# An adaLN transformer block on one core: conditioning vector loaded first, exponential table loaded early, one query in another PSUM bank, and one small task moved from head 17 to head 31

## Chip, cores, metric

The kernel runs on one core of a Trainium2 chip. The metric is the device time of one execution in microseconds. Each comparison with the kernel before is made on one chip, in the same rounds. "Clock" is the mean granted share of TensorE's clock over the run, rounded to three places: one stretch of 3.4 us at half clock makes it 0.999.

## The reference

```python
mod = silu(c) @ w_mod                     # c: (1, 1024); six vectors of 1024
sa, ca, ga, sb, cb, gb = ...
h = layernorm(x) * (1 + ca) + sa          # x: (2048, 1024), bf16
x = x + ga * attention(h)                 # 32 heads of 128, 4 kv heads, last 512 keys
h = layernorm(x) * (1 + cb) + sb
x = x + gb * swiglu(h)                    # 1024 -> 3584 -> 1024
```

## The kernel before

TensorE works through 4 chunks of 512 rows; in each chunk it makes the query of every head (8 matmuls), its scores (4), and scores times V (16), then the output projection in 8 pieces of 32 matmuls, and at the end the feed-forward part. Heads are counted through all chunks, 32 to a chunk, and the query of head `i + LEAD` (`LEAD` is 3) is made beside head `i`. VectorE copies results out of PSUM, ScalarE takes exponentials. Small jobs ("background tasks": layer norm of the next chunk, broadcasts of a vector into rows) are Python generators that advance one step per head. A tracker puts in the semaphore waits, per PSUM bank and per tile.

The opening. The vector `c` is the third transfer on SyncE's queue; its transpose is TensorE's first instruction:

```python
for t in range(TPC):                       # 4 tiles of x, on two queues in turn
    q = Q_xa[t // 2] if t % 2 else Q_x[t]
    T.op(q, lambda: (A if t % 2 else SP).dma_start(x_res[:, t, :], ...))
    if t == 2:
        T.op(Q_c, lambda: SP.dma_start(c_row[:, :], ...))
...                                        # (cut) weight transfers on SyncE
T.op(PE, ... TE.transpose(bank_bf(XB)[:, 0:DT], c_row, ident))
T.op(ACT, ... A.activation(sc_bf, ..., AF.Silu))
...                                        # (cut) statistics and normalised tiles
warm(9, WB); x_first(0); warm(4, WB); x_first(1)    # warm: matmuls on zeros
...                                        # (cut) modulation, x_first(2), x_first(3)
x_mod()                                    # cast of the modulation, scaled copies into hT
```

The first four queries are computed before the shift of the layer norm is known (a vector; VectorE's cast of it at 26.09 us in before); its contribution is a bias, summed up in bank 2 (`SCB + 2`) by one-column matmuls. The queries lie in `QB0 = [5, 6, 0, 4]`; the scores use banks 0 to 3, later queries bank 4 (`QB`), scores times V banks 5 and 6 (`PVB`), the small tasks and every second output-projection piece bank 7 (`XB`):

```python
T.op(DVE, ... V.tensor_copy(bq, psap((SCB + 2) * 512, ...)))  # copy the biases out of PSUM
q_out(0)               # VectorE: bank 5 + bq[0] -> query 0
q_out(2, True)         # ScalarE: bank 0 + bq[2] -> query 2
q_out(3, True)         # ScalarE: bank 4 + bq[3] -> query 3
for dt in range(5, DT): shift(dt)          # VectorE
q_out(1)               # VectorE
...
if i == 17:
    bg.insert(0, row_task(sc_row, B_scr, sc_bf[:, :], B_sc))
if i == 5:
    add_ln1(1)
...
if (i + LEAD) % Hq == 0:
    finish(ln1[(i + LEAD) // Hq])          # run background steps until it is done
qproj(i + LEAD)                            # always into bank QB
...
def oproj(ch):
    for k in range(2 * TPC):
        b = [QB, XB][k % 2]
        oproj_mm(ch, k, b, 0, Hq)          # 32 matmuls
        oproj_end(ch, k, b)                # two VectorE operations, then run_bg(1)
```

`row_task` has three steps: scale four identity tiles on POOL; four matmuls of 128 columns into bank 7 and a copy on VectorE; the same again for the second half.

The softmax here doesn't subtract the row's maximum and nothing guards it: scores larger than these inputs give would overflow.

## Time and profile before

| what | value | from |
|---|---|---|
| time | 1281.59 us median of 4 (1280.76 to 1282.10) | runs |
| matmuls on TensorE | 1267.8 of 1278.9 us, 99% | page |
| wait for the vector `c` | 6.0 us | chain |
| first scores of head 0 start | 28.68 us | timeline |
| wait before the sixth query | 0.56 us | timeline |
| distance of two query casts at the end of chunk one | 4.46 us; elsewhere 3.50 | timeline |

The first lines of the page of before: span, and busy time of each engine with its share of the span.

```profile
span 1278.9 us, 17849 instructions
...
PE 1267.8 (99%) x7650; PEld 644.5 (50%) x7650; DVE 477.3 (37%) x884; ACT 339.5 (27%) x383; POOL 41.8 (3%) x102
```

The chain of work that ended last in before, in order of time (start us, duration us, what). It shows the few places in which something other than TensorE sets the time.

```profile
1.64 4.35 DMA c_row<-in_c_dram
5.99 0.05 issue
6.04 0.18 PE ps L395
...
15.77 0.18 DVE mod_bf L470
...
27.60 0.16 DVE bq L670
27.76 0.02 issue
27.78 0.76 DVE arena L664
28.55 0.14 issue
28.68 2.76 PE ps L268 x12
31.45 0.02 issue
31.47 0.70 DVE arena L611
...
32.22 3.67 PE ps L268 x28
...
130.00 0.69 DVE arena L712
130.69 0.33 DVE arena L420
```

The vector lands at 5.99. The modulation is cast at 15.77; I use that cast as the mark for the end of the opening. The bias copy (27.60) and query 0 (27.78) release the first scores at 28.68. The cast of the fifth query (31.47) holds the sixth (32.22), which needs the same bank. At 130.69 a modulation of the layer norm holds the first query of chunk two.

VectorE's timeline of before around that last place (start, us, engine, line, operation, output<-input, count, and in brackets the idle time before):

```profile
128.01 0.69 DVE L611 CAST arena<-ps 128x512 bf16<-128x512 f32 x1 [0.17 <-PE ps L268]
...
130.60 1.38 DVE L420 TENSOR_SCALAR arena<-arena,gain,mod_bf 128x512 bf16<-128x512 bf16 x4
132.47 0.69 DVE L611 CAST arena<-ps 128x512 bf16<-128x512 f32 x1 [0.48 <-PE ps L268]
```

Four modulations (L420) come in one lump, and the query casts (L611) are 132.47 - 128.01 = 4.46 us apart. TensorE's wait for them shows as only 0.46 us of idle time; after it, three matmuls start 0.32 us apart instead of 0.216, in step with the remaining modulations.

ScalarE's timeline of before where the first exponential is:

```profile
27.78 1.26 ACT L661 ACTIVATE arena<-ps,bq 128x512 bf16<-128x512 f32 x2 [0.35 <-DVE bq L670]
29.07 1.28 ACT L691 ACT_TABLE_LOAD   x1
30.36 2.14 ACT L691 ACTIVATE arena<-ps 128x1024 bf16<-128x1024 f32 x2
```

### The profile page before, as it was taken

What the parts mean: (1) busy time and instruction counts of PE and PEld (TensorE: products, weight loads), DVE (VectorE), ACT (ScalarE), POOL (GpSimd) and SP (SyncE); (2) the same over time, 40 slices, a digit from 0 to 9 for tenths busy, and PEclk for the clock granted to TensorE, in tenths of its full rate; (3) what the DMA queues carried; (4) which work ended last, traced back from release to release, by engine and by line L of the source; (5) the groups of instructions that cost most, each with busy time, mean ns of one, the idle gap of its engine ahead of it and who ended that gap; (6) DMA issues with size and microseconds to landing.
All of it is one profiled execution on the core that took longest, in us unless ns stands there. A gap on an engine that the chain in (4) does not pass through costs nothing.

```text
span 1278.9 us, 17849 instructions
## 1 busy us (share of the span) xinstructions
PE 1267.8 (99%) x7650; PEld 644.5 (50%) x7650; DVE 477.3 (37%) x884; ACT 339.5 (27%) x383; POOL 41.8 (3%) x102
## 2 busy tenths in 40 slices
PE   7999999999999999999999999999999999999999
PEld 4565545655456564455654444444444444444444
DVE  4555324765237652265322321233222331221222
ACT  3555303555025550055510111011100111011100
POOL 1030000000000010000000000000000000000000
PEclk9999999999999999999999999999999999999999
DMA  9999403966008841055352964045421654035200
GB/s 326 227 237 236 104 1 68 204 137 162 9 20 181 158 104 42 1 130 115 71 149 77 292 224 132 19 146 165 134 73 43 198 147 132 17 114 166 67 9 25
DMA packets 234830, 155.31 MB, mean 121 GB/s; under 512 B 129024, under 2 KB 220032, under 8 KB 234752
## 3 DMA queue, kind: packets, MB, share of 16 engines
q1 hardware_dynamic: 176224, 94.93, 30.6%
q10 hardware_dynamic: 58528, 59.25, 14.7%
q8 instruction: 60, 0.98, 0.3%
q14 instruction: 18, 0.15, 0.0%
HBM read 119.54 MB, written 4.19 MB: 97 GB/s over the span
## 4 chain that ended last, share of the span: by engine, by line
PE 99%; DVE 0%; DMA 0%; issue 0%; SPq 0%
PE ps L268 99%; DMA c_row<-in_c_dram 0%; PE ps L272 0%; SPq L307 0%; DVE arena L664 0%; DVE arena L611 0%; DVE arena L712 0%; DVE tmp L731 0%; DVE arena L733 0%; DVE arena L476 0%; DVE arena L420 0%; DVE rl L709 0%; DVE gain L456 0%; PE ps L395 0%; DVE mod_bf L470 0%
## 5 line engine op out<-in xcount | busy, mean ns | idle before, releaser
L268 PE MATMUL ps<-arena 128*128 128x512 bf16 (+1 forms) x7377 | 1263.0, 334 | 2.2 <-DVE arena L664 0.7
L268 PEld LDWEIGHTS ps<-arena 128*128 128x128 bf16 x7377 | 635.2, 98 | 620.6 <-issue 2.8
L691 ACT ACTIVATE arena<-ps 128x1024 bf16<-128x1024 f32 x256 | 261.9, 1023 | 355.2 <-PE ps L268 343.4
L916 ACT ACTIVATE arena<-ps 128x512 bf16<-128x512 f32 x112 | 66.9, 597 | 506.5 <-PE ps L268 506.5
L917 DVE TENSOR_TENSOR arena<-ps,arena 128x512 bf16<-128x512 f32 x112 | 77.4, 691 | 276.2 <-PE ps L268 276.2
L731 DVE TENSOR_TENSOR tmp<-ps,rowb 128x512 f32<-128x512 f32 (+1 forms) x65 | 44.4, 683 | 319.1 <-PE ps L268 319.1
L611 DVE CAST arena<-ps 128x512 bf16<-128x512 f32 x124 | 85.8, 692 | 58.9 <-PE ps L268 58.9
L712 DVE TENSOR_TENSOR arena<-ps,rl 128x512 bf16<-128x512 f32 x128 | 88.5, 691 | 4.4
L709 DVE RECIPROCAL rl<-ps 128x4 f32<-128x4 f32 x128 | 23.4, 182 | 120.4 <-PE ps L268 120.4
L404 DVE BATCH_NORM_STATS2 st<-x_res 128x6 f32<-128x512 bf16 x62 | 42.3, 683 | 4.5 <-DMA x_res<-in_A_x_dram 4.4
L409 POOL TENSOR_SCALAR rstd<-mv 128x1 f32<-128x1 f32 x28 | 6.2, 221 | 920.0 <-DVE mv L408 920.0
L565 DVE SCALAR_TENSOR_TENSOR arena<-arena 128x1024 bf16<-128x1024 bf16 x24 | 29.2, 1215 | 0.0
L733 DVE TENSOR_TENSOR arena<-tmp,x_res 128x512 bf16<-128x512 f32 (+1 forms) x33 | 22.3, 676 | 1.1
L733 DVE TENSOR_TENSOR x_res<-tmp,x_res 128x512 bf16<-128x512 f32 x32 | 22.1, 692 | 1.1
L420 DVE TENSOR_SCALAR arena<-arena,gain,mod_bf 128x512 bf16<-128x512 bf16 x56 | 20.3, 406 | 0.0
L415 DVE TENSOR_SCALAR nsc<-x_res,mv,rstd 128x1024 bf16<-128x1024 bf16 x30 | 16.0, 535 | 0.0
L411 POOL TENSOR_TENSOR rstd<-rstd,mhalf 128x1 f32<-128x1 f32 x28 | 15.8, 564 | 2.3
L580 POOL TENSOR_SCALAR arena<-arena,c 128x128 bf16<-128x128 bf16 x24 | 14.1, 605 | 9.0 <-PE ps L268 8.8
L268 PEld LDWEIGHTS ps<-sc_bf,arena 128*128 128x128 bf16 x192 | 7.2, 96 | 3.2
L268 PE MATMUL ps<-sc_bf,arena 128*128 128x1 bf16 x192 | 7.3, 164 | 0.0
L408 DVE BATCH_NORM_AGGREGATE mv<-st 128x2 f32<-128x12 f32 x28 | 5.8, 209 | 1.0
L395 PE MATMUL ps<-arena,c_row 8*128 8x8 bf16 x1 | 0.2, 181 | 6.0 <-DMA c_row<-in_c_dram 6.0
(52 smaller groups left out, 42.7 us busy)
## 6 DMA issues: line engine op xcount, KB each, us to landing
arena<-in_A_wq_dram SPq DMA_DIRECT2D x31, 1024.0 KB, 5.7
arena<-in_B_w_gate_dram ACTq DMA_DIRECT2D x28, 1024.0 KB, 5.4
arena<-in_B_w_up_dram ACTq DMA_DIRECT2D x28, 1024.0 KB, 8.2
arena<-in_A_wo_dram SPq DMA_DIRECT2D x8, 1024.0 KB, 7.0
arena<-in_B_w_down_dram SPq DMA_DIRECT2D x7, 1024.0 KB, 8.0
out_dram<-arena SPq DMA_DIRECT2D x15, 256.0 KB, 2.0
x_res<-in_A_x_dram SPq DMA_DIRECT2D x3, 1024.0 KB, 6.7
arena<-in_w_mod_dram SPq DMA_DIRECT2D x8, 256.0 KB, 5.9
```

The lines of the kernel that those rows point to most:

```text
L268: T.op(PE, lambda: TE.matmul(out_ap, lhsT, rhs, start=start, stop=stop, skip_group_check=skip), reads=reads, writes=[bank_buf])
L404: T.op(DVE, lambda: V.bn_stats(st_[sl][:, hf * 6:hf * 6 + 6], x_res[:, t, hf * 512:hf * 512 + 512]), reads=[B_x[t]], writes=[B_st[sl]])
L420: T.op(DVE, lambda: V.tensor_scalar(dst[:, dt, :], dst[:, dt, :], gain[gi][:, dt:dt + 1], mod_bf[:, ccol + dt:ccol + dt + 1], op0=ALU.mult ...
L565: T.op(DVE, lambda: V.scalar_tensor_tensor(mt[n % 2], mt[n % 2], 1.0, sc_row, op0=ALU.mult, op1=ALU.mult, accum_out=mcol[:, n:n + 1]), rea ...
L611: T.op(DVE, lambda: V.tensor_copy(qT_s[qs], bank(QB)), writes=[PB[QB], B_qT[qs]])
L691: T.op(ACT, lambda: A.activation(ex_s[es][:, 2 * kp:2 * kp + 2, :], banks2(SCB + 2 * kp), AF.Exp, scale=att_scale), writes=[PB[SCB + 2 * k ...
L709: T.op(DVE, lambda: V.reciprocal(rl[r][:, :].rearrange("p (a b) -> p a b", a=2), psap(PVB * 512 + P, [[512, 2], [130, 2]])), writes=both + ...
L712: T.op(DVE, lambda: V.tensor_tensor(o_s[os_].rearrange("p (a b) d -> p a b d", a=2), psap(PVB * 512, [[512, 2], [130, 2], [1, P]]), rlb, A ...
L731: T.op(DVE, lambda: V.tensor_tensor(tmp[s][:, 0:n], bank(b, n), rowb[ri][:, c0:c0 + n], ALU.mult), reads=[B_row[ri]], writes=[PB[b], B_tmp ...
L733: T.op(DVE, lambda: V.tensor_tensor(dst[:, c0:c0 + n], tmp[s][:, 0:n], x_res[:, t, c0:c0 + n], ALU.add), reads=[B_tmp[s], B_x[t]], writes= ...
L916: T.op(ACT, lambda: A.activation(sg_s[ss], bank(gb), AF.Silu), writes=[PB[gb], B_sg[ss]])
L917: T.op(DVE, lambda: V.tensor_tensor(guT[:, ft, :], bank(ub), sg_s[ss], ALU.mult), reads=[B_sg[ss]], writes=[PB[ub], B_gu[ft]])
```

## The change

The intent is to shorten the opening and to take small waits off TensorE: the vector goes first on ScalarE's queue, with two warm-up matmuls ahead of its transpose; the exponential's table is loaded in a pause of ScalarE; query 0 reads its bias straight from PSUM, ahead of the bias copy; the sixth query goes to bank 5; the row task that is first needed at head 38 starts at head 31 instead of 17.

```diff
-    Q_c = dq("q_c")
+    Q_c = dq("q_c", nc.scalar)
...
+            T.op(Q_c, lambda: A.dma_start(c_row[:, :], ...), writes=[B_cT])
             for t in range(TPC):
...
-                if t == 2:
-                    T.op(Q_c, lambda: SP.dma_start(c_row[:, :], ...), writes=[B_cT])
...            (the transpose of c and its Silu move down, behind two warm-up matmuls)
+            warm(2, WB)
...
+            T.op(ACT, lambda: A.activation(acc[:, 0:1], mhalf[:, 0:1], AF.Exp), ...)
...
-            warm(9, WB)
+            warm(8, WB)
...
             def q_out(h, on_act=False):
-                if on_act:
+                if h == 0:
+                    T.op(DVE, lambda: V.tensor_scalar(qT_s[h], bank(QB0[h]), bank(SCB + 2, 1, 2 * h), None, op0=ALU.add),
+                         writes=[PB[QB0[h]], PB[SCB + 2], B_qT[h]])
+                elif on_act:
...
+            q_out(0)
             T.op(DVE, lambda: V.tensor_copy(bq[:, :], psap((SCB + 2) * 512, ...)), ...)
-            q_out(0)
...
-                if i == 17:
+                if i == 31:
                     bg.insert(0, row_task(sc_row, B_scr, sc_bf[:, :], B_sc))
...
-                    qproj(i + LEAD)
+                    qproj(i + LEAD, PVB if i == 2 else QB)
```

More of the change, by code (lines that the diff above doesn't have):

```diff
@@ L235, in bass_adaLN_cond__sliding_block_cached__swiglu_ffn__prompt_kernel @@
     B_mode = _Buf("mode"); B_modc = _Buf("modc"); B_bq = _Buf("bq"); B_gf = _Buf("gf")
-    B_nm = _Buf("nmean"); B_acc = _Buf("acc")
+    B_nm = _Buf("nmean"); B_acc = _Buf("acc"); B_acc0 = _Buf("acc0")
     B_g = [_Buf("g%d" % i) for i in range(2)]
@@ L304, in _ @@
             Q_xa = [dq("q_xa%d" % i, A) for i in range(2)]
+            T.op(Q_c, lambda: A.dma_start(c_row[:, :], c.rearrange("o (k p) -> (o k) p", p=P)), writes=[B_cT])
             for t in range(TPC):
@@ L307, in _ @@
                 T.op(q, lambda: (A if t % 2 else SP).dma_start(x_res[:, t, :], xf[t * P:(t + 1) * P, :]), writes=[B_x[t]])
-                if t == 2:
-                    T.op(Q_c, lambda: SP.dma_start(c_row[:, :], c.rearrange("o (k p) -> (o k) p", p=P)), writes=[B_cT])
             OFF_WO = 0
@@ L392, in _ @@
             T.op(POOL, lambda: g.memset(v_aug[:, :, P:P + 2], 1.0), writes=[B_va])
-            T.op(PE, lambda: TE.transpose(bank_bf(XB)[:, 0:DT], c_row[:, :], ident[0:DT, 0:DT]),
-                 reads=[B_cT, B_ident], writes=[PB[XB]])
-            T.op(ACT, lambda: A.activation(sc_bf[:, :], bank_bf(XB)[:, 0:DT], AF.Silu), writes=[PB[XB], B_sc])
             B_ns4 = B_ns + [_Buf("ns2"), _Buf("ns3")]
@@ L485, in mod_ca @@
                 mod_mm(wca[k], B_wca[k], k, MCOLS)
+            WB = PVB
+            warm(2, WB)
+            T.op(PE, lambda: TE.transpose(bank_bf(XB)[:, 0:DT], c_row[:, :], ident[0:DT, 0:DT]),
+                 reads=[B_cT, B_ident], writes=[PB[XB]])
+            T.op(ACT, lambda: A.activation(sc_bf[:, :], bank_bf(XB)[:, 0:DT], AF.Silu), writes=[PB[XB], B_sc])
             tl = TPC - 1
@@ L490, in _ @@
                  reads=[B_x[tl]], writes=[B_ns4[tl], B_acc])
-            WB = PVB
             def stats_only(t):
@@ L509, in _ @@
                  reads=[B_x[tl], B_nm], writes=[B_ns4[tl], B_acc])
+            T.op(ACT, lambda: A.activation(acc[:, 0:1], mhalf[:, 0:1], AF.Exp), reads=[B_mh, B_nm], writes=[B_acc0])
             norm(0, 0, 0)
@@ L600, in _, with qproj @@
             Q_tr = [dq("q_tr%d" % i) for i in range(NOS)]
-            def qproj(i):
+            def qproj(i, b=QB):
                 ch, h = divmod(i, Hq)
@@ L607, in qproj @@
                 for kc in range(DT):
-                    mm(bank(QB), wq_s[sl][:, kc, hh * P:(hh + 1) * P], hT[ch % 2][:, kc, :], kc == 0, kc == DT - 1,
-                       [B_wq[sl][kc // HK], B_hT[ch % 2][kc]], PB[QB])
+                    mm(bank(b), wq_s[sl][:, kc, hh * P:(hh + 1) * P], hT[ch % 2][:, kc, :], kc == 0, kc == DT - 1,
+                       [B_wq[sl][kc // HK], B_hT[ch % 2][kc]], PB[b])
                 qs = i % NQT
-                T.op(DVE, lambda: V.tensor_copy(qT_s[qs], bank(QB)), writes=[PB[QB], B_qT[qs]])
+                T.op(DVE, lambda: V.tensor_copy(qT_s[qs], bank(b)), writes=[PB[b], B_qT[qs]])
             QB0 = [PVB, PVB + 1, SCB, QB]
```

## The prediction

> **What bounds it.** TensorE: the page shows its matmuls busy 1267.8 of 1278.9 us (99%) at granted clock 1.0, and the chain that ended last is 99% TensorE. About 11 us are idle, 6.0 of them before the first instruction, a transpose waiting for the conditioning vector. No matmul work is removed, so over 2% (25 us) is out of reach; what counts is starts and stalls of about a microsecond (timelines of before).
>
> **Gains**
>
> 1. Opening. The vector, issued third at 1.64 us, lands at 5.99; first on ScalarE's queue (0.73) it should land near 3. Warm-up starts near 2.2. The row-tile transposes then wait not for TensorE (9.66) but for VectorE's tiles: first ready at 8.03, second at 10.01, fourth at 12.43. The second tile's transposes start near 10.0 instead of 11.1, the scaled copies near 14.7 instead of 15.77: **-1.1**. Input tiles 1 and 3 are issued 0.4 us later, within slack (landed 4.61 and 5.79, needed 6.01 and 6.33). Weights landed early enough (first query weights 13.45).
> 2. Sixth query in its own bank: the 0.56 us wait (in all 31.49 to 32.22) for the cast out of the shared bank goes: **-0.7**.
> 3. Row task away from head 17: it took three background slots from the second chunk's layer norm, so four modulations were forced out at 130.60 and TensorE stalled; two query casts stand 4.46 us apart there instead of 3.50: **-0.95**.
> 4. Exponential table: its 1.28 us load (29.07 to 30.35) leaves the place before the first exponential, but the next scores come at 33 us and would not have waited: **0**. (The Trainium skill, "ScalarE: Activation LUTs", What ACT_TABLE_LOAD costs, gives 1283 ns plus a drain; this trace agrees on 1.28 and shows no drain.)
>
> **Losses**
>
> 5. First query before the bias copy. The first scores write bank 0, which holds the third query; ScalarE evacuates that with the copied bias. The copy ends about 0.78 us later (behind a 0.75 us operation), so bank 0 is free at about 29.2 instead of 28.4; the first query, earlier by 0.19, no longer decides. Scores start near 29.35 instead of 28.68 (before the opening's shift): **+0.65**.
> 6. Row task at head 31: its third step falls after the first of eight output-projection pieces. Its four small matmuls write the bank that the second piece uses; VectorE must first do two residual operations (0.69 each), then the row copy (0.68). TensorE idles from about 155.3 to 157.3 (before's times): **+1.95**, where before has nothing.
>
> **Sum**: -1.1 -0.7 -0.95 +0.65 +1.95, about -0.2: **1281.8 us** against 1282.04; range 1280.2 to 1283.4. Chances: faster by over 2% 0.003, within 2% 0.994, slower 0.003.
>
> **The profile should show** the first transpose near 3 us; scaled copies from 14.4 to 15.0; no wait before the sixth query; the first scores held by ScalarE's bias evacuation of the third query; the table load near 10 us; query casts 3.5 us apart to the end of chunk one; a new 2 us hole after the first output-projection piece, ended by the row copy.
>
> **What would make it wrong.** TensorE now idles about 1.6 us between warm-up and the first row tiles (6.4 to 8.0). In before the clock rose at 9.33 us, 3.3 us after TensorE started. The Trainium skill ("TensorE: Matmul & The Clock Gate", Part 1) tells of a free-running window of about 3.4 us; the trace agrees with that length. Should the window straddle that pause, the opening's matmuls run at half speed and up to 1.5 us of step 1 is lost, differently from run to run. Or input tile 0, alone at first, lands 0.3 us earlier and speeds VectorE's chain. If the row task's third step is cheaper than I reckon, the kernel is 2 us faster.

## The result, and the profile after

The median is 1281.34 us (1280.08 to 1282.21, 4 runs) against 1281.59 us (1280.76 to 1282.10, 4 runs). The ratio is 0.9998 with a 95% interval of 0.9981 to 1.0015. (Ratios are the mean time of one kernel's fast runs over that of the other's of the same rounds, so not quite the ratio of the medians quoted.) The four runs fall on two levels: 1280.08 and 1280.53 at clock 1.0, and 1282.15 and 1282.21 at clock 0.999. The profiled run is one of the latter.

The chain of the profile after, same columns:

```profile
1.76 6.47 DMA x_res<-in_A_x_dram
...
14.54 0.18 DVE mod_bf L464
...
26.37 0.76 DVE arena L661
27.13 0.02 issue
27.15 0.16 DVE bq L674
27.31 0.80 DVE arena L656 x3
28.11 4.34 PE ps L268 x12
...
154.40 0.70 DVE tmp L734
155.10 0.02 issue
155.13 0.69 DVE x_res L736
155.82 0.61 DVE arena L588
156.43 0.05 issue
156.48 1121.15 PE ps L268 x6360
```

The opening ends at 14.54 instead of 15.77. The bias copy now comes behind query 0 (27.15 behind 26.37). The first scores start only 0.59 us earlier than in before, and then 12 matmuls take 4.34 us that took 2.76. At 154.40 there is a new piece of chain: two residual operations and a row copy (L588), one after the other, before TensorE goes on at 156.48.

TensorE's timeline after, at the first scores and at the new hole, with the idle time in brackets:

```profile
25.90 0.81 PE L268 MATMUL ps<-arena 128*128 128x512 bf16 x3
28.09 4.36 PE L268 MATMUL ps<-arena 128*128 128x512 bf16 x12 [1.38 <-DVE arena L656]
...
156.48 33.84 PE L268 MATMUL ps<-arena 128*128 128x512 bf16 x156 [1.89 <-DVE arena L588]
```

The clock of the profile after in two neighbouring windows (stretch, length, busy time and number of instructions of TensorE, its weight loads, VectorE, ScalarE and GpSimd, PEclk, DMA share, GB/s):

```profile
24.54:27.95 3.41, 2.17 (x41) 1.16 (x38) 2.86 (x10) 1.81 (x4) 0.00 (x0) 1.00 1.11 359
27.95:31.36 3.41, 3.27 (x8) 1.19 (x9) 0.81 (x2) 2.71 (x4) 0.00 (x0) 0.50 0.84 210
```

TensorE's clock is halved for exactly one stretch of 3.41 us, right behind the stretch that holds the 1.38 us pause. Eight matmul records lie in it; the same 3.41 us hold 19 where the clock stayed up (run with the row task at head 27, below).

VectorE's timeline after, at the end of chunk one and at the hole:

```profile
128.02 0.69 DVE L611 CAST arena<-ps 128x512 bf16<-128x512 f32 x1 [0.82 <-PE ps L268]
...
131.51 0.69 DVE L611 CAST arena<-ps 128x512 bf16<-128x512 f32 x1 [0.82 <-PE ps L268]
...
154.40 0.69 DVE L734 TENSOR_TENSOR tmp<-ps,rowb 128x512 f32<-128x512 f32 x1 [6.00 <-PE ps L268]
155.13 0.69 DVE L736 TENSOR_TENSOR x_res<-tmp,x_res 128x512 bf16<-128x512 f32 x1
155.74 0.68 DVE L588 CAST arena<-ps 128x512 bf16<-128x512 f32 x1
163.60 0.69 DVE L734 TENSOR_TENSOR tmp<-ps,rowb 128x512 f32<-128x512 f32 x1 [7.18 <-PE ps L268]
```

The casts are 3.49 us apart, so the stall of before is gone; but the first two residuals are 163.60 - 154.40 = 9.20 us apart, where before has 6.90 (155.13 and 162.03).

Following the same marks through the two profiles gives the whole difference. "Step" is how much the lead of the changed kernel moves between two marks.

| mark | before | after | after - before | step | what happened in it |
|---|---|---|---|---|---|
| cast of the modulation | 15.77 | 14.54 | -1.23 | -1.23 | opening |
| cast of the shift vector | 26.09 | 24.86 | -1.23 | 0 | |
| first scores | 28.68 | 28.09 | -0.59 | +0.64 | bank 0 freed later |
| cast of the seventh query | 37.88 | 38.33 | +0.45 | +1.04 | half clock, less the sixth query's wait |
| cast at 128 us | 128.01 | 128.02 | +0.01 | -0.44 | row task's 8 matmuls no longer here |
| next cast | 132.47 | 131.51 | -0.96 | -0.97 | stall at head 29 gone |
| first residual | 155.13 | 154.40 | -0.73 | +0.23 | first half of the row task |
| second residual | 162.03 | 163.60 | +1.57 | +2.30 | second half of the row task and the hole |
| residual at the very end | 1276.09 | 1277.65 | +1.56 | 0 | 1100 us without a difference |

### The profile page after: what moved, and what is told of

It is laid out like the page before. It is cut to its first block, busy times and chain, and to the rows that moved or that the text cites. A ratio compares the mean times of both kernels' runs of the same rounds, so it can differ in the third digit from the quotient of the medians.

```text
span 1280.4 us, 17849 instructions
## 1 busy us (share of the span) xinstructions
PE 1270.6 (99%) x7651; PEld 645.0 (50%) x7651; DVE 477.3 (37%) x884; ACT 339.8 (27%) x384; POOL 41.8 (3%) x102
## 4 chain that ended last, share of the span: by engine, by line
PE 99%; DMA 1%; DVE 0%; ACT 0%; POOL 0%; ACTq 0%; issue 0%; DVEq 0%
PE ps L268 98%; DMA x_res<-in_A_x_dram 1%; PE ps L272 0%; ACT arena L490 0%; DVE tmp L734 0%; DVE arena L656 0%; DVE arena L661 0%; DVE x_res L736 0%; DVE arena L588 0%; ACTq L305 0%; POOL rstd L499 0%; DVE arena L409 0%; DVE arena L736 0%; DVE arena L470 0%; ACTq L308 0%
## 5 line engine op out<-in xcount | busy, mean ns | idle before, releaser
L272 PE MATMUL ps<-arena 128*128 128x128 bf16 x32 | 2.8, 219 | 0.3 <-DVE arena L409 0.3
```

## The experiments

In each round the kernel before ran beside the experiments: 1280.80 us median of 9 runs in the first set, 1281.08 of 7 in the second, 1281.34 of 9 in the third. All experiments gave correct results.

**Row task at head 27, in front of the queue.** Is the hole the row copy?

```diff
-                if i == 31:
+                if i == 27:
                     bg.insert(0, row_task(...))
```

> The changed kernel with the row task at head 27 instead of 31. My theory (the 1.9 us hole after the first output-projection piece is the row copy queued behind VectorE's residual operations for the bank of the second piece): the hole goes, the next residual starts about 6.9 us after the first instead of 9.2, query casts stay 3.5 us apart to the end of the first chunk, and the time falls by 1.9 us against the changed kernel at full clock, to about 1278.4. Rival (the second piece waits there for something else, such as a weight or the last transposed head, and VectorE merely ends last): a hole of over 1 us remains between the first two pieces and the time falls by under 0.7 us.

Measured: 1280.36 to 1280.72 us in three runs, and 1281.91 and 1282.38 in two (the last at clock 0.999). The residuals are 6.90 us apart: the hole is gone. The time is not lower, though, because my edit made a new wait. TensorE's waits in this kernel between 100 and 200 us (engine and line, waited for: us, times, longest):

```profile
PE ps L268 <- DVE arena L588: 1.5, 1, 1.5
PE ps L268 <- POOL arena L580: 0.4, 1, 0.4
```

At head 29 the layer norm is finished by force, by running steps from the front of the queue. The layer norm had made its last step but was still in the list, behind the row task, so the whole row task was run at once in front of the query. Two query casts are 6.35 us apart there. The hole belongs to the row copy; the expected time failed by my edit.

**Row task at head 27, behind the layer norm.**

```diff
-                if i == 31:
-                    bg.insert(0, row_task(...))
+                if i == 27:
+                    bg.append(row_task(...))
```

> The changed kernel with the row task at head 27, but put behind the layer-norm task instead of in front of it, so that the forced finish of the layer norm at head 29 does not drag the row task along (which made the wait of 2.4 us in the run before with head 27). Theory (hole = row copy behind residuals; wait at head 29 = forced tasks): neither wait shows, TensorE has no idle time between 100 and 200 us, query casts 3.5 to 3.75 us apart, residuals 6.9 us apart; 1.9 us less than the changed kernel at full clock, 1278.3 to 1278.6. Rival (some other cost of moving the task): a wait of 1 us or more remains in 100 to 200 us.

Measured: 1278.14 us median (1277.98 to 1278.58, 4 runs, all at clock 1.0), ratio 0.9978 (0.9963 to 0.9993). Between 100 and 200 us TensorE has no wait at all; query casts are 3.50 to 3.72 us apart, residuals 6.90. The time is 0.2 below the expected range at its median. So the hole and its 1.9 to 2.1 us were avoidable: the task fits between the end of the layer norm and the output projection.

**Row task back at head 17.**

```diff
-                if i == 31:
+                if i == 17:
```

> The changed kernel with the row task at head 17 as in the kernel before: the other parts of the change alone. Theory: no hole after the first output-projection piece (residuals 6.9 us apart), but the stall at the end of chunk one is back (two query casts 4.46 us apart instead of 3.50). Net 0.9 to 1.0 us less than the changed kernel at full clock: 1279.2 to 1279.5. Rival (the stall of before had another cause than the task's three slots): casts stay 3.50 apart, 1278.3.

Measured: 1278.94, 1279.04 and 1279.09 us at clock 1.0, and 1280.58 at 0.999. The casts are 4.46 us apart again, the residuals 6.91. The move to head 31 thus took away a stall of 0.96 and put a larger one in its place. The three full-clock times are 0.1 to 0.3 below the expected range.

**Bias copy first, query 0 reading the copy.**

```diff
-            q_out(0)
             T.op(DVE, lambda: V.tensor_copy(bq, ...))
+            q_out(0)        # and q_out(0) takes bq[:, 0:1] as in before
```

> The changed kernel with the bias copy first again and the first query reading the copy. My theory (the first scores wait for ScalarE to free bank 0, which waits for the copy): the scores start 0.65 us earlier after the cast of the shift vector (24.86 in the changed kernel's profile, so 3.2 to 2.6 us after it), TensorE's idle before them falls from 1.4 to 0.75 us; the time at full clock falls by 0.6 us against the changed kernel. Rival (the profile's attribution, VectorE's shift of the last columns, decides): the scores move by under 0.2 us. On the clock: the changed kernel lost it for one 3.4 us window after the 1.4 us pause in its profile and in 2 of 4 runs shows 0.999; with the shorter pause the 0.999 should be rarer.

Measured: 1279.94 us median (1279.36 to 1281.43, 5 runs, none at 0.999). TensorE's timeline:

```profile
25.30 0.81 PE L268 MATMUL ps<-arena 128*128 128x512 bf16 x3
26.86 2.75 PE L268 MATMUL ps<-arena 128*128 128x512 bf16 x12 [0.75 <-DVE arena L667]
```

The cast of the shift vector starts at 24.27, so the scores start 2.59 us after it (before: 2.59; after: 3.23). The order alone makes the 0.64 us, in the amount foreseen; the fastest run is 0.7 below the changed kernel's fastest (1280.08). The profile after names VectorE's shift (L656) for this wait, but that is ruled out: these shifts start 2.37 us after the cast of the shift vector in the profile after and 2.36 us here, and the scores moved all the same. The view names what came last by the profile, and the shifts merely ended at that time.

**First scores in the order of banks 1, 3, 2, 0.**

```diff
-                for kt in range(KT):
+                for kt in (1, 3, 2, 0) if i == 0 else range(KT):
...
-                for kp in range(KT // 2):
+                for kp in (1, 0) if i == 0 else range(KT // 2):
```

> The changed kernel with the four score matmuls of the first head in the order of banks 1, 3, 2, 0, and the exponentials of banks 2 and 3 first. If ScalarE's evacuation of bank 0 is what holds the first scores, the first score matmul now starts when the first query is ready, 0.8 to 0.9 us earlier (about 2.4 us after the cast of the shift vector starts, instead of 3.2), though the last one still waits for bank 0; time at full clock lower by about 0.6 us (three of four matmuls, 0.65 us, move into the pause). Rival (VectorE's shift decides): the first score stays where it was, no gain. The pause is shorter, so a granted clock of 0.999 should be rarer than half of the runs.

Measured: 1280.32 us median (1280.00 to 1281.36, 5 runs, none at 0.999). TensorE's timeline:

```profile
27.11 1.22 PE L268 MATMUL ps<-arena 128*128 128x512 bf16 x4 [0.56 <-DVE arena L661]
28.60 1.89 PE L268 MATMUL ps<-arena 128*128 128x512 bf16 x8 [0.28 <-ACT arena L664]
```

The first score comes 2.41 us after the cast of the shift vector (24.70), as expected, and that it can do so without bank 0 confirms that bank 0 was the hold. But the time hardly moved: the next eight matmuls make query 4 in bank 4, which ScalarE frees last. They start 3.90 us after that cast; in the changed kernel at full clock it is 4.09 (27.56 plus four matmuls of 0.215, minus 24.33, in the run with head 27). The gain of 0.6 was wrong; the wait moved on to the next bank, and 0.2 was left.

**Nine idle-filling matmuls before the first scores instead of three.**

```diff
-            warm(3, SCB + 3)
+            warm(9, SCB + 3)
```

> The changed kernel with nine instead of three idle-filling matmuls ahead of the first scores, which covers TensorE's 1.4 us pause there without moving the scores by over 0.1 us. If the two levels of the changed kernel's time (1280.1 to 1280.5 at clock 1.0, 1282.2 at clock 0.999) come from the clock gate judging a window that holds this pause, no run should show 0.999, and all runs lie at about 1280.3. Rival (the lost window comes by chance or from the pauses in the opening): about half of the runs still show 0.999 and 1282.

Measured: 1280.08, 1280.21, 1280.26, 1280.45 and 1280.93 us, all at clock 1.0. The scores still start 3.23 us after the cast of the shift vector. The count over all experiments is clearer than this one. Kernels that keep the 1.38 us pause (the changed one, the three with a moved row task, the ones with one bank and without the early exponential) show 0.999 in 8 of 25 runs. Kernels in which the pause is filled or at most 0.75 us long show it in 0 of 29, and none of the 25 runs of before in these three sets does. In all four profiles that lost the clock, it had risen at 7.17 to 7.75 us and fell 20.48 us later, six times 3.413: at 27.65 to 28.23, between 0.14 us before and 0.67 us after the end of the pause. In the two full-clock profiles with the same pause the clock had risen at 5.04 and 5.43; counted on in the same way, the window that holds the pause goes on for 1.4 and 1.8 us of dense matmuls after it. So not the pause alone decides, but how a window falls on it. Nor does the idle time in that window decide. Counted from the rise, one window holds the whole pause in a profile that lost the clock (row task at 17, the first line) and in one that kept it (row task at 27, behind the layer norm, the second line); columns as above:

```profile
24.24:27.65 3.41, 2.03 (x38) 1.12 (x37) 3.18 (x11) 2.14 (x4) 0.00 (x0) 1.00 1.11 355
25.52:28.93 3.41, 2.03 (x10) 0.78 (x9) 2.44 (x7) 2.15 (x4) 0.00 (x0) 1.00 0.97 257
```

TensorE is busy for 2.03 us in both. In the three lost windows of this kind 0.55 to 0.81 us of that are one-column matmuls; in the two kept ones all of it is 512-column matmuls. The profile of this experiment even kept the clock through a window in its opening (5.91 to 9.33) with 1.40 us idle in two gaps, and with no one-column matmul in it. This fits one-column matmuls counting for less than 512-column ones. It is not shown: no experiment varied them, and in the two kept windows the pause also ends earlier before the window does (1.4 and 1.8 us, against 0.2 to 0.7). The Trainium skill ("TensorE: Matmul & The Clock Gate", Part 1) tells of a free-running window of 3413 ns; the trace agrees, with its half-clock stretches of 3.413 us and with 20.48 us as six of them.

**The vector first, alone.** The kernel before with only the queue of `c` and the two warm-up matmuls changed.

```diff
-    Q_c = dq("q_c")
+    Q_c = dq("q_c", nc.scalar)     # and first in the queue; warm(2), transpose, ..., warm(8)
```

> The kernel before with the conditioning vector first on ScalarE's queue and the two warm-up matmuls ahead of its transpose, nothing else of the change. Theory: the cast of the shift vector comes at 24.3 to 24.9 us instead of 26.09 (1.2 to 1.8 earlier), the first scores 2.6 us after it as in before, the waits at the sixth query and at head 29 stay; lowest times 1.2 us below the kernel before's lowest 1280.6, about 1279.4. Rival (the opening is bound by something else by then and gives the gain back before the scores): the first scores come less than 0.6 us earlier than 28.68.

Measured: 1279.02 us median (1278.81 to 1279.27, 4 runs, clock 1.0), ratio 0.9984 (0.9967 to 1.0000). The shift vector's cast is at 24.70 and the first scores at 27.29, 2.59 later. The waits of 0.56 and 0.46 us at the sixth query and at head 29 stay. This one part is faster than the whole change: its slowest run is below the changed kernel's fastest (1280.08), though in other rounds. Its lowest time is 0.6 below the 1279.4 expected.

**The sixth query in the shared bank again.**

```diff
-                    qproj(i + LEAD, PVB if i == 2 else QB)
+                    qproj(i + LEAD)
```

> The changed kernel with the sixth query in the shared bank again. Theory: TensorE waits 0.56 us before the sixth query's matmuls for the cast of the fifth; the casts of fifth and sixth query lie 2.69 us apart as in before instead of 1.95; time 0.7 us above the changed kernel at equal clock. Rival (the wait moves to the next scores, which wait for the exponentials anyway): casts 2.69 apart but the next ones (seventh) at the same distance from the fifth as in the changed kernel (5.84 us at full clock there), no difference in time.

Measured: 1280.66, 1280.84 and 1281.10 us at clock 1.0, 1282.48 at 0.999. The casts of query five, six and seven are 2.69 and 3.72 us apart, 6.41 in all; in the changed kernel at full clock 1.95 and 3.89, 5.84 in all. So the bank saves 0.57, not the 0.74 of the first distance. The 0.17 that comes back later fits the use of bank 5 by scores times V right after, which now waits for the cast of the sixth query; that cause is only argued.

**Without the early exponential.**

```diff
-            T.op(ACT, lambda: A.activation(acc[:, 0:1], mhalf[:, 0:1], AF.Exp), ...)
```

> The changed kernel without the exponential in the opening: the table load comes back before the first real exponential. Theory: that exponential starts 1.2 to 1.3 us later after the bias evacuations, but TensorE's matmuls keep their distances (casts of fifth and sixth query 1.95 us apart, the seventh 3.9 after the sixth), no difference in time at equal clock: 1280.1 to 1280.7, and 1282 where the clock shows 0.999. Rival (the exponentials are on the chain there): the sixth-to-seventh distance grows by up to 1 us, and the time with it.

Measured: 1280.13 us at clock 1.0; 1281.78, 1282.25 and 1283.05 at 0.999. ScalarE's timeline:

```profile
26.81 1.27 ACT L663 ACTIVATE arena<-ps,bq 128x512 bf16<-128x512 f32 x2 [1.14 <-DVE bq L673]
28.10 1.28 ACT L693 ACT_TABLE_LOAD   x1
29.39 2.14 ACT L693 ACTIVATE arena<-ps 128x1024 bf16<-128x1024 f32 x2
```

The casts are 1.95 and 3.89 us apart with or without the table load in this place. The early load is worth nothing here. That three of four runs lost the clock instead of one in four I take for chance, but no run here proves it.

**The parts put together.** Bias copy first, row task appended at head 27, six idle-filling matmuls.

> The changed kernel with the bias copy first again, the row task at head 27 behind the layer norm, and six instead of three idle-filling matmuls ahead of the first scores (they fill the 0.75 us pause that is left). If the parts add up: 1.95 us less for the hole and 0.64 less for the first scores than the changed kernel at full clock (1280.1 to 1280.5), so 1277.5 to 1277.9, no run at clock 0.999, all runs within about 1 us. Against the kernel before, about 3.2 us or 0.25% less: within the 2% that counts as the same. If the parts don't add up (one wait hides another): 1278.1 or more.

Measured: 1277.31 us median (1277.27 to 1277.77, 5 runs, all at clock 1.0), ratio 0.9970 (0.9958 to 0.9983). It is faster than both kernels, by 0.3% against before. The median is 0.2 below the expected range; the parts add up.

**The same with input tile 3 on SyncE's queue.**

```diff
-                q = Q_xa[t // 2] if t % 2 else Q_x[t]
-                ... (A if t % 2 else SP).dma_start(x_res[:, t, :], ...)
+                q = Q_xa[0] if t == 1 else Q_x[t]
+                ... (A if t == 1 else SP).dma_start(x_res[:, t, :], ...)
```

> The combined kernel with the fourth input tile issued on SyncE's queue, third there, ahead of the weights, instead of third on ScalarE's. In all kernels with the vector first that tile landed at 7.0 to 8.2 us, not at 5.8 as before, because the weights issued meanwhile on the other queue share the transfer engines; it sets ScalarE's mean and through POOL the third and fourth normalised tile. Theory: it lands before 6.2 us, TensorE's wait before the third tile's transposes goes, the first cast of the modulation comes at 13.8 to 13.9 us in the profile (13.91 to 14.54 in the other kernels); up to 0.4 us less than the combined kernel and less spread. Rival (weights, one issue later, now hold TensorE): the cast comes no earlier than 13.9.

Measured: 1277.33 us median (1277.30 to 1277.80, 5 runs): no difference, and no less spread (1277.27 to 1277.77 without this part). ScalarE's first use of the tile:

```profile
5.72 1.06 ACT L490 ACTIVATE arena<-x_res 128x1024 bf16<-128x1024 bf16 x1 [2.19 <-DMA x_res<-in_A_x_dram]
```

The tile is used at 5.72 instead of 8.10 us, so the part about the transfer holds. But the modulation is cast at 13.91 us, no earlier than in the best of the other profiles (13.91 with the row task at 17). (In the profile of the combined kernel it is 14.38, but that is its slowest run, 1277.77.) By then something else holds the opening: in this profile's chain TensorE works without a wait from 9.10, just after VectorE has the second normalised tile ready, to 13.88. The expected gain did not come.

**The kernel before, profiled again**, because its own times spread by 1.8 us at clock 1.0.

> The kernel before, unchanged, profiled once more. Its times spread from 1280.4 to 1282.1 us although every run shows clock 1.0, and the kernel with only the vector moved spreads by 0.5 us. If that spread comes from the place in which the clock gate's window falls while the opening's matmuls run, this profile's clock rises elsewhere than at 9.33 us, and the first cast of the modulation moves with it: later than 15.77 us by about half of what the rise is later, and the time above 1280.7 by as much; if the clock rises at 9.3 or earlier the time is 1280.4 to 1280.8. Rival: the time differs by 0.5 us or more from that with the same rise.

Measured: 1281.35 us, clock 1.0. In the first profile of before (1280.66 us) the clock rose at 9.33 us, in this one at 10.71, 1.38 later. VectorE's cast of the modulation:

```profile
16.45 0.17 DVE L470 CAST mod_bf<-ps 128x8 bf16<-128x8 f32 x1 [4.00 <-PE ps L268]
```

It is 0.68 us later than 15.77, half of 1.38, and the time is 0.69 us longer. VectorE's second normalised tile starts at 9.52 and 9.54 us in the two, so the input did not make the difference. So in before the opening runs at half clock until a window ends (the matmuls start 0.427 us apart before the rise, 0.215 after it), and where that falls sets the time, as far as two profiles tell. (The mean clock does not show it: the records begin with the rise.) In the profile with the vector first alone, the clock rises at 5.94, before the first row tile's transposes (7.10), and the four runs of that kernel lie within 0.5 us. It is not always so: with the bank order changed it rose at 8.28.

## Why the prediction was right

The forecast of 1281.8 us (1280.2 to 1283.4), with nearly all of the chance on the same time within 2%, holds: 1281.34 us. It was not right because nothing happened. Three gains (0.6 to 1.2 us) and two losses (0.6 and 2.1) nearly cancel, as it said; with the measured sizes (-1.23, -0.57, -0.96, +0.64, +2.1) the sum is about 0 instead of -0.2. That the two medians then agree with it so closely is partly luck, as the first and the last point show. Point by point:

- *Opening, -1.1*: -1.23 in the profile (-1.2 to -1.9 in all profiles with the vector first). The vector's transpose ran at 3.13 us. That the size came out is partly luck, because two errors offset each other. Input tile 0 came so much earlier that VectorE's first statistics start at 3.57 instead of 4.43 us; the prediction has this, with 0.3 us, only among what would make it wrong. So the second tile's transposes start at 9.22, not near 10.0, and 1.75 earlier than in before (10.97). And the slack did not cover input tile 3. It landed at 8.23 us instead of 5.79, because weights were being issued on SyncE's queue from 1.65 us, ahead of this tile's 1.76. The Trainium skill ("DMA: Bandwidth & Descriptors", Issuing engines are not separate DMA queues) says that transfers from all issuers interleave on the same 16 engines; this agrees, 8.23 against 5.7 when the tile was issued ahead of the weights. TensorE waits 0.29 us for what follows from it, and the third tile's transposes start at 11.38, only 1.28 earlier than in before (12.66).
- *Sixth query, -0.7*: 0.74 at the place, 0.57 in all.
- *Row task away from head 17, -0.95*: 0.96.
- *Exponential table, 0*: 0.
- *Query 0 before the bias copy, +0.65*: 0.64; putting the copy first took exactly this away.
- *Row task at head 31, +1.95*: the hole is 1.89 us of idle time. The two halves of the task and the hole cost 2.53 there, less the 0.44 saved at head 17, so 2.1.
- *What would make it wrong*: the danger was the right one, a pause of TensorE under the window of the clock gate. The place was wrong. I feared the pause at 6.4 to 8.0 us in the opening. It struck at the 1.38 us pause before the first scores, which step 5 itself lengthens from 0.75. That cost 1.6 us in 2 of 4 runs (half clock in the profile; the two levels are 1.6 to 2.1 us apart). The sum left this out; it is the largest term missed. In the medians it may be offset by something else left out: before pays for the phase of the same window in its opening, 0.69 us in the second profile. At its best state the changed kernel stands at 1280.1 to 1280.5 against before's 1280.4 to 1280.8, about 0.3 lower, near the 0.2 that the sum gave (few runs, and not of the same rounds). I also set the 3.3 us from TensorE's start to the rise beside the window's length; in the second profile of before it is 4.65 (6.06 to 10.71), so that agreement was chance, and it is the half-clock stretches of 3.413 us that show the length.

What stays open: what a window must hold to keep the clock. The one that lost it in the profile after (24.54 to 27.95) held 1.24 us of the pause and 32 one-column matmuls; the comparison of windows above shows that the idle time alone does not decide, and no more. It also stays open why single runs at clock 1.0 lie 1.4 to 2.1 us above the fastest of their kernel (1281.91 with the row task at 27, 1281.43 with the copy first, 1281.36 with the bank order changed): none of these was profiled.

## What to carry to other kernels

A kernel whose main engine is 99% busy can still be moved by a few tenths of a per cent through small tasks, but each moved task needs a look at what stands around its new place: which bank it writes, who uses that bank next, and what lies ahead of its copy in the copying engine's queue. When an operation is moved to the front, find out who waited for the one that it passed; here the passed bias copy fed the evacuation of the bank that the next matmuls needed. And when one kernel's times fall on two levels, look at the clock records before you compare medians: the level at 0.999 shows in none of the 15 runs in which dummy matmuls filled the pause before the first scores (1.4 us of it in 5 runs, 0.75 in 10).

## What the Trainium skill lacked or had wrong

- "TensorE: Matmul & The Clock Gate", Why this matters for your kernels, advises no idle gaps over about 3 us. Here a gap of 1.38 us cost the clock in 8 of 25 runs, for one window of 3.413 us and about 1.6 us of time; with gaps of at most 0.75 us in that place it was 0 of 29. The idle time alone did not decide: two profiles kept the clock through a window with the whole 1.38 us in it. Its section on PSUM-queue cycling tells of frequent short gaps, but no page has a single gap well under one window that does this.
- The same page, Part 1, has the free-running window; it does not say that the window's phase can be followed through a trace. Here the clock fell exactly 20.48 us, six windows, after it rose, in four profiles out of four that lost it.
- The same page puts the cost of the ramp at the start under 1% of a typical kernel's span. That is so here, but its phase made the difference between two profiles of one kernel: clock up 1.38 us later, time 0.69 us longer, more than the effect of the change.
- "ScalarE: Activation LUTs", What ACT_TABLE_LOAD costs, gives 1283 ns plus a drain of about 1380 ns for every switch. The load is 1.28 us here, but no drain shows: the evacuation ends at 28.08 us, the load runs from 28.10, and the exponential starts at 29.39.
